# Reordering the first batch's bank reads and moving loads between DMA queues, in a spectral filter and gated feed-forward kernel

## The chip, the cores and the metric

The kernel runs on one core of a Trainium2 chip. A core has a matrix engine (TensorE, PE in the profile), VectorE (DVE), ScalarE (ACT), GpSimd (POOL) and SyncE (SP), and 16 DMA engines that SP, ScalarE and GpSimd feed through queues of their own (SP's and ScalarE's are q1 and q10 in the profile, GpSimd's q0). The metric is the device time of one execution in microseconds (us); the time of a kernel is the median of its runs.

## The reference

`x` has 8 batches of 3008 rows of 256 values. Each column is filtered in the frequency domain, and the result goes, row by row, through a gated feed-forward block with 1536 hidden columns:

```python
X = np.fft.rfft(x, axis=1)
y = np.fft.irfft(X * (filt_r + 1j * filt_i)[None], n=3008, axis=1)
t = y.reshape(8 * 3008, 256)
out = (np.maximum(t @ w_gate, 0) * (t @ w_val)) @ w_out
```

## The kernel before, in words

The sequence of 3008 is factored as 94 x 32, and the transform becomes matrix products in three stages.

**Stage A** is a transform of length 94, an fp32 product with the table `WA`. For batch 0 it is `first_a`, whose result VectorE transposes into `AT`. For batch 1 it is `items_a`: 16 items, four to each of four parts c. Each item is one product into a bank `psA` and one copy into `asb`; after four items a part is stored to the DRAM buffer `Abuf`. Batch 1's `Abuf` is then read back by `load_at`, in four parts, as the tile `at`. Batches from 2 on do stage A in another way (`load_chunk`, `fold_chunk`, `tiled_a`), which the change leaves alone.

**Stage B** works in six steps i. `fwd` makes two banks `psX` (e = 0 and 1). `product` multiplies each bank with the real and with the imaginary filter table (`Ftr` for k = 0, giving `tt`; `Fti` for k = 1, giving `uu`), four products to a step. `inv` turns `tt` and `uu` of a step into two banks `psD`, and copies them into `dsb`, which goes in a few stores to the DRAM buffer `Dbuf`. For seven of the 24 products of batch 0, listed in `POOL_U`, ScalarE first copies the bank into an fp32 tile `xs` and GpSimd multiplies that copy; VectorE does the rest from the bank. Within step i the order written out is `fwd(i)`, `inv(i-2)`, the products, and then what `amid(i)` puts in: some of the items A of batch 1, taken one by one from the generator `early`.

**Stage C** (`item_c`) reads `Dbuf` back in four slabs z (`load_d`, tile `dC`), multiplies with `M1`, and gives `yT`, a block of 512 rows of the filtered sequence, transposed.

**The feed-forward loop** takes 47 blocks of 512 rows. For each block there are 12 steps `gv` with the products `psV` and `psG` (L485), a copy of `psV` by ScalarE (L488) and a product by VectorE (L490). `o_part` multiplies the block before with `WoT` (L504). From here on, the work of the other stages is hung at given steps of the loop by `at_step`.

Each engine takes its instructions in the order in which the program writes them. Loads into the weights `WvT`, `WgT` and `WoT` go by GpSimd's queue (`load_vg`, by columns, and `load_o`). `hold_gpsimd` is a tiny copy on GpSimd that reads some tile; what stands behind it on GpSimd is held until that tile is written. Half of each filter table's rows are a copy of the other half (`place_filter`, made with an engine's copy or with a DMA).

Before the feed-forward loop starts the program writes, in order: the first B with its items A, `load_d` of slabs 0 and 1, a hold of GpSimd until slab 0 is there, the second half of `WvT` and `WgT`, the items A that are left with `item_c` of block 0 among them, a hold until `yT` is there, `WoT`. `load_at` of batch 1 is at steps 0 to 3 of the loop, slabs 2 and 3 at steps 9 and 14, all on SP's queue.

Of the kernel before, what the change touches and what calls it, by code (L numbers as in the profile page):

```python
# [35 lines left out]
def _ap(t, offset_elems, ap_list):  # L36
    return dataclasses.replace(
        t, offset=t.offset + offset_elems, ap=[list(p) for p in ap_list]
    )
# [81 lines left out]
def kernel(  # L121
# [10 lines left out]
    nc = tc.nc  # L132
    B, S_, D = x.shape
    DFF = moe_w_gate.shape[1]
# [4 lines left out]
    NZ = 4  # L139
# [95 lines left out]
    def place_filter(fi, a, half, copy):  # L235

        dst = FILT[fi][1]
        gs = slice(H * half, H * half + H)
        r = a * 64
        copy(dst[r + 32:r + 64, gs, :], dst[r:r + 32, gs, :])  # L240

    def place_nyq():
        for (src, dst), n in zip(FILT, nyq):
            nc.vector.tensor_copy(dst[96:97, NG - 1, :], n)

    def load_vg(c0, c1):
        for (w_hbm, w_sb) in ((moe_w_val, WvT), (moe_w_gate, WgT)):
            nc.gpsimd.dma_start(w_sb[:, :, c0:c1],
                                _ap(w_hbm, c0, [[DFF, 128], [128 * DFF, 2], [1, c1 - c0]]))

    def load_o():
        for c in range(2):
            nh = NFT // 2
            nc.gpsimd.dma_start(WoT[:, c * nh:(c + 1) * nh],
                                _ap(moe_w_out, c * nh * 128 * D, [[D, 128], [128 * D, nh], [1, D]]))

    def hold_gpsimd(tile_):

        scr = sb.tile([128, 8], FP32, tag="scr", bufs=2)
        nc.gpsimd.tensor_copy(scr[:tile_.shape[0]], tile_)  # L260
# [101 lines left out]
    POOL_U = ((0, 1), (1, 0), (1, 1), (2, 0), (2, 1), (3, 1), (4, 0))  # L362
    ats = {}

    def load_at(b, c):
        if c == 0:
            ats[b] = sb.tile([128, NG, D], BF16, tag="at", bufs=1, name="at")
        nc.sync.dma_start(ats[b][c:c + 125:4],
                          _ap(Abuf[b], c * NROW * NC2 * D, [[D, 32], [4 * NC2 * D, NG], [1, D]]))

    psXs, tus, dsbs = {}, {}, {}
# [15 lines left out]
    def product(b, i, e, k, pool=False):  # L387

        psX = psXs[b, i, e]
        pool_, bufs = (fs, 4) if b else (pro, 6)  # L390
        p = pool_.tile([128, 2, D], BF16, tag=("tt", "uu")[k], bufs=bufs, name=("tt", "uu")[k])
        filt = (Ftr, Fti)[k][:, 4 * i + e:4 * i + 4:2, :]
        if pool:
            xs = pro.tile([128, 2, D], FP32, tag="xs", bufs=3)
            nc.scalar.copy(xs, psX)
            nc.gpsimd.tensor_tensor(p, xs, filt, op=ALU.mult)
        else:
            nc.vector.tensor_tensor(p, psX, filt, op=ALU.mult)  # L398
        tus[b, i, e, k] = p

    def inv(b, i, tags=None, cuts=CUTS):

        if i in cuts:
            dsbs[b] = i, sb.tile([128, 2, 4, D], BF16, tag="dsb", bufs=3, name="dsb")
        i0, dsb = dsbs[b]
        psD = [ps.tile([128, 2, D], FP32, tag=tags[a] if tags else fft_tag(), name="psD")
               for a in range(2)]
        for m in range(2):
            for k in range(2):
                for a in range(2):  # L410
                    for e in range(2):
                        nc.tensor.matmul(psD[a][64 * e:64 * e + 64, m],  # L412
                                         (I2t, I2u)[k][64 * a:64 * a + 64, 4 * i + 2 * m + e, :],
                                         tus[b, i, e, k][64 * a:64 * a + 64, m],
                                         start=(k == 0), stop=(k == 1),
                                         tile_position=(64 * a, 64 * e))
        o = 2 * (i - i0)
        for a in range(2):
            nc.scalar.copy(dsb[:, a, o:o + 2, :], psD[a])  # L419
        if i + 1 in cuts:  # L420
            nc.sync.dma_start(_ap(Dbuf[b], 2 * i0 * D, [[NG * D, 128], [NG // 2 * D, 2], [1, (o + 2) * D]]),
                              dsb[:, :, :o + 2, :])

    def first_b(amid):

        cuts = (0, 2, 4, 5, 6)
        for i in range(6):
            fwd(0, i)
            if i > 1:
                inv(0, i - 2, cuts=cuts)  # L430
            for e in range(2):
                product(0, i, e, 0)
                product(0, i, e, 1, pool=(i, e) in POOL_U)
            amid(i)
        inv(0, 4, cuts=cuts)
        amid(6)
        inv(0, 5, cuts=cuts)

    dCs = {}

    def load_d(b, z0=0, z1=NZ):
        for z in range(z0, z1):
            dC = sb.tile([NROW, 8, D], BF16, tag="dC", bufs=6)
            for e in range(2):
                nc.sync.dma_start(dC[48 * e:48 * e + 48],
                                  _ap(Dbuf[b], (64 * e + 16 * z) * NG * D,
                                      [[D, 48], [48 * D, 8], [1, D]]))
            dCs[b, z] = dC
# [13 lines left out]
    def item_c(k, h):  # L462

        if h == 0:
            yTs[k] = sb.tile([128, 2, W], BF16, tag="yT", bufs=3, name="yT")
        tag = fft_tag() if k == 0 else ("psv", "psg")[h]
        psY = ps.tile([128, W], FP32, tag=tag, name="psY")
        for (o, b, n2, n1, w) in runs(k * W, W):
            nc.tensor.matmul(psY[:, o:o + w],  # L469
                             dCs[b, n2 // 8][:, n2 % 8, h * 128:(h + 1) * 128], M1[:, n1:n1 + w],  # L470
                             start=True, stop=True)
        dst = yTs[k][:, h]
        if h == 0:
            nc.scalar.copy(dst, psY)  # L474
        else:
            nc.vector.tensor_copy(dst, psY)  # L476
# [57 lines left out]
    def warm(n, cols=512):  # L534

        psJ = ps.tile([128, 512], FP32, tag=fft_tag(True), name="psJ")
        for i in range(n):
            nc.tensor.matmul(psJ[:, :cols], junk[:, 0:128], junk[:, :cols], start=True, stop=True)
# [36 lines left out]
        turn_a(h)  # L575
    for i in range(12):
        warm(2)
    place_filter(1, 1, 0, nc.scalar.copy)
    place_filter(1, 0, 0, nc.vector.tensor_copy)
    for half in range(2):  # L580
        for a in range(2):
            place_filter(0, a, half, nc.sync.dma_start)
# [8 lines left out]
    def amid(i):  # L591
        if i == 3:
            place_nyq()
        for _ in range((1, 1, 1, 2, 1, 2, 1)[i]):
            next(early)()

    hold_gpsimd(AT[0:32, NG - 1, D - 8:])
# [1 line left out]
    turn["tags"], turn["side"] = ("fft", "psv", "psg"), "pso"  # L599
    first_b(amid)  # L600
    turn["tags"], turn["side"] = ("fft", "psv", "psg", "pso"), None
    load_d(0, 0, 2)
    hold_gpsimd(dCs[0, 0][:, 7, D - 8:])
    for c in range(2, 4):
        load_vg(c * DFF // 4, (c + 1) * DFF // 4)
    for i, f in enumerate(early):
        f()
        if i == 5:
            for h in range(2):
                item_c(0, h)  # L610
    hold_gpsimd(yTs[0][:, 0, 0:8])
    load_o()
    prologue.close()
    fs = ctx.enter_context(tc.tile_pool(name="fs", bufs=2))
    XP = []
# [9 lines left out]
    def at_step(s, f):  # L625
        side.setdefault(s, []).append(f)

    for s, z in ((9, 2), (14, 3)):
        at_step(s, lambda z=z: load_d(0, z, z + 1))
    C_AT = (8, 10)  # L630
    at_step(2, clear_chunks)
    for b in range(1, B):
        end = (b * S // W - 1) * NFT + C_AT[0] - 5
        if b == 1:
            for c in range(4):
                at_step(c, lambda c=c: load_at(1, c))
        else:
            for j, e in enumerate((-74, -69, -62, -55) if b == 2 else (-74, -69, -64, -57)):
                l = (22, 29, 34, 43)[j] if b == 2 else end - 115 + NFT * j

                def next_x(b=b, j=j, l=l):
                    hold_gpsimd(prods[-1][:, 0:8])
                    load_chunk(b, j)
                    if j:
                        fold_chunk(b, j - 1)
                    if j == 3:
                        fold_chunk(b, j)
                at_step(l, next_x)
                at_step(end + e, lambda b=b, j=j: tiled_a(b, j))
            at_step(end + e + 4, lambda b=b: load_at_tiled(b))  # L650
        for i in range(7):
            l = -35 + 5 * i if b == 1 else -40 + 6 * i
            if i < 6:
                at_step(end + l, lambda b=b, i=i: fwd(b, i))
                for h in range(4):
                    at_step(end + l + h, lambda b=b, i=i, h=h: product(b, i, h // 2, h % 2))
            if i > 0:
                at_step(end + l, lambda b=b, i=i: inv(b, i - 1, ("psv", "psg")))
        at_step(end - 2, lambda b=b: load_d(b))
# [42 lines left out]
```

## Time and profile before

| | |
|---|---|
| median of 3 runs | 891.98 us (891.27 to 892.26) |
| the profiled execution's own time | 891.01 us |
| its span | 889.2 us |
| TensorE busy | 866.7 us, 97% |
| VectorE, ScalarE, GpSimd busy | 572.9, 500.0 and 365.3 us |
| mean granted clock of TensorE | 0.997 |

The profile is of one execution. Its span runs from the first to the last instruction, and the execution's own time has 1.8 us around it. Busy shares are averages over the whole span. What a change in one stage is worth is read from that stage, so most readings here are of the stretch from 20 to 80 us, in which the first B ends and the feed-forward loop begins.

### The profile page before, as it was taken

How to read it: one execution, taken by the hardware profiler on the slowest of the kernel's cores; microseconds unless marked ns; L12 is line 12 of the kernel's file. 1: busy time of each engine (PE TensorE's matmuls, PEld its weight loads, DVE VectorE, ACT ScalarE, POOL GpSimd, SP SyncE). 2: the span in 40 equal slices, each digit the busy share in tenths (PEclk: the TensorE clock that was granted, in tenths of full speed). 3: DMA queues.
4: the chain of work that ended last, by engine and by line, in shares of the span. 5: the costliest groups of instructions: out<-in, count | busy, mean ns of one | idle time of the engine just before them, and what ended most of it. 6: DMA issues, size and time to landing. Idle time of an engine off the chain costs nothing.

```text
span 889.2 us, 18975 instructions
## 1 busy us (share of the span) xinstructions
PE 866.7 (97%) x7065; PEld 506.8 (57%) x7186; DVE 572.9 (64%) x871; ACT 500.0 (56%) x889; POOL 365.3 (41%) x361
## 2 busy tenths in 40 slices
PE   8889999999999999999999999999999999999997
PEld 3335555556556665566655665556555556566665
DVE  4837766577666776667765676657776577655553
ACT  4655555555655566556565556555655555555553
POOL 4450697138651577316771176802867000000001
PEclk9999999999999999999999999999999999999999
DMA  9994556534556337453376334763446512321111
GB/s 242 289 234 83 158 138 154 128 104 118 130 139 134 105 101 157 125 124 96 106 184 133 84 104 110 176 138 82 118 134 149 122 31 80 89 67 36 37 31 53
DMA packets 110769, 107.26 MB, mean 121 GB/s; under 512 B 20167, under 2 KB 95463, under 8 KB 110038
## 3 DMA queue, kind: packets, MB, share of 16 engines
q1 hardware_dynamic: 86998, 78.20, 34.5%
q0 software_dynamic: 22960, 26.40, 12.1%
q10 hardware_dynamic: 720, 1.45, 0.5%
q8 instruction: 56, 0.92, 0.4%
q14 instruction: 35, 0.29, 0.1%
HBM read 60.42 MB, written 48.23 MB: 122 GB/s over the span
## 4 chain that ended last, share of the span: by engine, by line
PE 86%; DVE 4%; ACT 4%; DMA 3%; issue 2%; POOL 0%; SPq 0%; DVEq 0%; POOLq 0%; ACTq 0%
PE psG L485 27%; PE psO L504 25%; PE psV L485 25%; DVE prod L490 3%; PE psF L341 3%; ACT vsb L488 3%; PE psD L412 2%; PE psX L382 2%; PE psY L469 2%; DMA Ftr<-Ftr 1%; DMA Ftr<-in_filt_r_dram 1%; PE psA L294 1%; DMA dC<-Dbuf 1%; DMA XF<-in_x_dram 1%; ACT dsb L419 0%
## 5 line engine op out<-in xcount | busy, mean ns | idle before, releaser
L490 DVE SCALAR_TENSOR_TENSOR prod<-psG,vsb 128x512 bf16<-128x512 f32 x564 | 389.3, 690 | 263.4 <-ACT vsb L488 254.5
L488 ACT CAST vsb<-psV 128x512 bf16<-128x512 f32 x564 | 332.3, 589 | 262.9 <-PE psV L485 176.5
L485 PE MATMUL psG<-yT,WgT 128*128 128x512 bf16 x1107 | 331.0, 379 | 6.9 <-DVE prod L490 0.8
L504 PE MATMUL psO<-WoT,prod 128*128 128x256 bf16 x2256 | 336.4, 273 | 1.1
L485 PE MATMUL psV<-yT,WvT 128*128 128x512 bf16 x1030 | 315.8, 380 | 0.5 <-ACT asb L348 0.5
L504 PEld LDWEIGHTS <-prod 128*128 128x128 bf16 x2256 | 220.6, 98 | 143.5
L485 PEld LDWEIGHTS <-WgT 128*128 128x128 bf16 x1128 | 110.1, 98 | 136.5 <-issue 3.6
L485 PEld LDWEIGHTS <-WvT 128*128 128x128 bf16 x1128 | 98.8, 98 | 42.3 <-issue 31.1
L260 POOL CAST scr<-prod 128x8 f32<-128x8 bf16 x24 | 4.6, 191 | 256.4 <-DVE prod L490 256.4
L527 POOL DMA_DIRECT2D out_dram<-osb x5 | 2.6, 538 | 195.9 <-ACT osb L517 195.9
L517 ACT COPY osb<-psO 128x512 f32<-128x512 f32 x92 | 54.0, 586 | 27.9 <-PE psO L504 26.5
L398 DVE TENSOR_TENSOR tt<-psX,Ftr 128x512 bf16<-128x512 f32 x96 | 65.1, 682 | 0.9 <-PE psX L382 0.9
L327 POOL TENSOR_TENSOR fold<-XP 128x1024 f32<-128x1024 f32 x24 | 56.5, 2356 | 19.7 <-PE psF L341 19.5
L398 DVE TENSOR_TENSOR uu<-psX,Fti 128x512 bf16<-128x512 f32 x89 | 60.6, 681 | 0.0
L419 ACT CAST dsb<-psD 128x512 bf16<-128x512 f32 x96 | 51.6, 589 | 13.1 <-PE psD L412 13.1
L314 POOL DMA_DIRECT2D XP<-in_x_dram x96 | 56.9, 598 | 3.0 <-PE psY L469 1.5
L328 POOL TENSOR_TENSOR XP<-XP 128x1024 f32<-128x1024 f32 x24 | 56.4, 2350 | 1.9
L348 ACT CAST asb<-psF 128x512 bf16<-128x512 f32 x48 | 25.8, 589 | 30.5 <-PE psF L341 30.5
L348 DVE CAST asb<-psF 128x512 bf16<-128x512 f32 x48 | 30.9, 686 | 18.6 <-PE psF L341 18.6
L474 ACT CAST yT<-psY 128x512 bf16<-128x512 f32 x47 | 27.6, 586 | 26.4 <-PE psY L469 26.2
L469 PE MATMUL psY<-M,dC 96*128 96x94 bf16 (+18 forms) x604 | 37.5, 198 | 4.1 <-DMA dC<-Dbuf 4.0
L476 DVE CAST yT<-psY 128x512 bf16<-128x512 f32 x47 | 32.0, 681 | 11.6 <-PE psY L469 11.6
(76 smaller groups left out, 492.4 us busy)
## 6 DMA issues: line engine op xcount, KB each, us to landing
dC<-Dbuf SPq DMA_DIRECT2D x64, 192.0 KB
XP<-in_x_dram POOLq DMA_DIRECT2D x48, 256.0 KB, 6.0
Dbuf<-dsb SPq DMA_DIRECT2D x23, 512.0 KB
at<-Abuf SPq DMA_DIRECT2D x28, 384.0 KB
XP<-in_x_dram POOLq DMA_DIRECT2D x96, 96.0 KB, 2.7
Abuf<-asb SPq DMA_DIRECT2D x96, 96.0 KB
out_dram<-osb SPq DMA_DIRECT2D x69, 94.0 KB
XF<-in_x_dram SPq DMA_DIRECT2D x15, 256.0 KB
```

Source lines behind the costliest of these rows:

```text
L314: nc.gpsimd.dma_start(xp[r:r + 24, 0:4:2, :], _ap(x, (b * N1 * N2 + o) * D, [[N2 * D, 24], [47 * N2 * D, 2], [1, 512]]))
L327: tt(t, xp[:, 0:2], xp[:, 2:4], op=ALU.add)
L328: tt(xp[:, 2:4], xp[:, 0:2], xp[:, 2:4], op=ALU.subtract)
L348: copy(asf[:, :, q, :], banks[q])
L398: nc.vector.tensor_tensor(p, psX, filt, op=ALU.mult)
L419: nc.scalar.copy(dsb[:, a, o:o + 2, :], psD[a])
L469: nc.tensor.matmul(psY[:, o:o + w], dCs[b, n2 // 8][:, n2 % 8, h * 128:(h + 1) * 128], M1[:, n1:n1 + w], start=True, stop=True)
L485: nc.tensor.matmul(pt[:, :W], w[:, h, ft * 128:(ft + 1) * 128], yt[:, h, :], start=(h == 0), stop=(h == 1))
L488: nc.scalar.copy(vsb, psV[:, :W])
L490: nc.vector.scalar_tensor_tensor(prod, in0=psG[:, :W], scalar=0.0, in1=vsb, op0=ALU.max, op1=ALU.mult)
L504: nc.tensor.matmul(psO[:, t % 2], prods[ft][:, t * 128:(t + 1) * 128], WoT[:, ft, :], start=(ft == 0), stop=(ft == NFT - 1))
L517: copy(osb[:, t0 % 2:t % 2 + 1], psO[:, t0 % 2:t % 2 + 1])
```

## The change

Six edits go together.

1. One of the four copies that fill the lower half of `Fti` for the first half of the columns (`place_filter(1, 0, 0)`) is made by a DMA on ScalarE's queue; VectorE made it.
2. In a step of the first B, the order of the four products depends on which of them GpSimd makes. Where it makes one of a bank, ScalarE's copy `xs` of that bank is written first and VectorE's product from the bank after it, where the two share a bank.
3. In the last step of the first B, the copy of `psD` for a = 0 is made by VectorE; ScalarE made both.
4. `amid(6)` no longer takes an item A. One more is left for after the first B, and `item_c` of block 0 comes after seven of these where it came after six.
5. The third quarter of `WvT` and `WgT` and the first part of `at` are loaded by GpSimd's queue at the end of step 5 of the first B.
6. After the first B only slab 0 goes by SP's queue. Slab 1, the last quarter of `WvT` and `WgT`, the second part of `at`, `WoT`, the third and fourth parts of `at`, and slabs 2 and 3 go by GpSimd's queue in this order, with a hold ahead of slab 1 (until slab 0 is there) and one ahead of `WoT` (until `yT` is there).

```diff
     def load_at(b, c):
...
-        nc.sync.dma_start(ats[b][c:c + 125:4],
+        nc.gpsimd.dma_start(ats[b][c:c + 125:4],
...
         for a in range(2):
-            nc.scalar.copy(dsb[:, a, o:o + 2, :], psD[a])
+            copy = nc.vector.tensor_copy if (b, i, a) == (0, 5, 0) else nc.scalar.copy
+            copy(dsb[:, a, o:o + 2, :], psD[a])
...
-            for e in range(2):
-                product(0, i, e, 0)
-                product(0, i, e, 1, pool=(i, e) in POOL_U)
+            on_pool = [(i, e) in POOL_U for e in range(2)]
+            seq = {(0, 0): ((0, 0), (0, 1), (1, 0), (1, 1)), (0, 1): ((1, 1), (0, 0), (0, 1), (1, 0)),
+                   (1, 0): ((0, 1), (1, 0), (1, 1), (0, 0)), (1, 1): ((0, 0), (1, 1), (0, 1), (1, 0))}
+            for e, k in seq[tuple(map(int, on_pool))]:
+                product(0, i, e, k, pool=k == 1 and on_pool[e])
...
-    def load_d(b, z0=0, z1=NZ):
+    def load_d(b, z0=0, z1=NZ, eng=nc.sync):
...
-                nc.sync.dma_start(dC[48 * e:48 * e + 48],
+                eng.dma_start(dC[48 * e:48 * e + 48],
...
+    place_filter(1, 0, 0, nc.scalar.dma_start)
     place_filter(1, 1, 0, nc.scalar.copy)
-    place_filter(1, 0, 0, nc.vector.tensor_copy)
...
-        for _ in range((1, 1, 1, 2, 1, 2, 1)[i]):
+        if i == 5:
+            load_vg(DFF // 2, 3 * DFF // 4)
+            load_at(1, 0)
+        for _ in range((1, 1, 1, 2, 1, 2, 0)[i]):
...
-    load_d(0, 0, 2)
+    load_d(0, 0, 1)
     hold_gpsimd(dCs[0, 0][:, 7, D - 8:])
-    for c in range(2, 4):
-        load_vg(c * DFF // 4, (c + 1) * DFF // 4)
+    load_d(0, 1, 2, nc.gpsimd)
+    load_vg(3 * DFF // 4, DFF)
     for i, f in enumerate(early):
         f()
-        if i == 5:
+        if i == 6:
             for h in range(2):
                 item_c(0, h)
+    load_at(1, 1)
     hold_gpsimd(yTs[0][:, 0, 0:8])
     load_o()
+    for c in range(2, 4):
+        load_at(1, c)
+    load_d(0, 2, 4, nc.gpsimd)
...
-    for s, z in ((9, 2), (14, 3)):
-        at_step(s, lambda z=z: load_d(0, z, z + 1))
...
-        if b == 1:
-            for c in range(4):
-                at_step(c, lambda c=c: load_at(1, c))
-        else:
+        if b > 1:
```

## The prediction, made before the result was known

> **What bounds the kernel now.** The page comes first: TensorE is busy nearly everywhere.
>
> ```profile
> PE 866.7 (97%) x7065; PEld 506.8 (57%) x7186; DVE 572.9 (64%) x871; ACT 500.0 (56%) x889; POOL 365.3 (41%) x361
> PE   8889999999999999999999999999999999999997
> ```
>
> The feed-forward loop starts with L485 at 57 us; after that TensorE's waits are small (waits by engine: 1.2 us in 56 to 130, 0.8 us later). All the changed code runs before or just after that start. So the end moves by as much as the first psV moves, plus whatever new wait appears in the first dozen steps. The chain of waits around that start:
>
> ```profile
> 43.83 1.05 ACT dsb L419 x2
> 44.88 0.55 ACT asb L297
> ...
> 45.45 1.07 ACT dsb L419 x2
> ...
> 46.54 2.43 DMA Dbuf<-dsb
> ...
> 49.06 0.33 SPq L445
> ...
> 49.44 5.09 DMA dC<-Dbuf
> ...
> 54.66 0.62 PE psY L469 x12
> 55.28 1.78 PE psA L294 x2
> 57.06 0.85 PE psV L485 x2
> ```
>
> The order is: last copy of the first B (to 46.52), store of D, load of D's first slab (to 54.53), psY, one item A, psV. TensorE runs out of items A at 50.7 and idles 3.97 us. The table of windows (sum, then PE, PEld, DVE, ACT and POOL busy, granted clock, DMA share, GB/s) shows the after-effect:
>
> ```profile
> 51.80:55.20 3.40, 0.54 (x13) 0.57 (x14) 0.00 (x0) 0.11 (x1) 0.28 (x2) 1.00 1.21 231
> 55.20:58.60 3.40, 3.18 (x9) 1.03 (x8) 0.69 (x1) 1.30 (x3) 3.40 (x6) 0.50 1.20 280
> 58.60:62.00 3.40, 3.40 (x17) 1.50 (x16) 2.29 (x4) 2.16 (x5) 3.40 (x4) 1.00 1.28 237
> ```
>
> The clock column is to be seen: one stretch of 3.4 us at 0.50. In it the item took 1.78 us instead of 0.9 and the first psV 0.85 instead of 0.43; with 0.22 of issue the price is about 1.5 us.
>
> Inside the first B the timeline shows who reads a bank first:
>
> ```profile
> 30.63 3.07 DVE L398 TENSOR_TENSOR tt<-psX,Ftr 128x512 bf16<-128x512 f32 x5
> 31.35 0.59 ACT L395 COPY xs<-psX 128x512 f32<-128x512 f32 x1 [3.71 <-DVE tt L398]
> 33.22 0.30 PE L412 MATMUL psD<-uu,I2u 64*64 64x256 bf16 x3 [0.94 <-POOL uu L396]
> ```
>
> ScalarE's xs waited 3.71 us for VectorE's tt on the same bank, GpSimd started late, and TensorE waited 0.94 us for its uu. A second such wait, 0.66 us for xs, comes at 35.87.
>
> **What the Trainium skill says.** "PSUM — Partial Sum Buffer", section "PSUM bank collisions raise a hardware error": two engines must not access one bank and quadrant together, reads included. The trace agrees (xs at 31.35, tt's end at 31.31). So in the new order VectorE waits for ScalarE where ScalarE waited before. "DMA: Bandwidth & Descriptors", section "Issuing engines are not separate DMA queues": all queues share 16 engines and interleave. Partly agreed: in 54 to 58.5 us SP's queue took 120.5% and none of GpSimd's packets, although GpSimd issued at 55.11; a GpSimd load starts late beside a full SP queue. "TensorE: Matmul & The Clock Gate", part 1: an idle window of about 3.4 us halves the clock, and the window is free-running. The trace agrees: 0.50 for 3.4 us.
>
> **The change part by part.** Spacings from the timeline: VectorE 0.60 us, ScalarE 0.48 in a run, GpSimd's product 1.16, an item A 1.03 and each further one 0.86, the 16 matmuls of inv 0.56.
>
> *Filter copy to ScalarE's queue.* VectorE's copy (28.45, 0.95 us) goes; the first tt comes at 28.92, when psX is there, instead of 29.43. ScalarE issues one DMA, about 0.55 us like SP's Ftr<-Ftr, after its last AS copy (23.53), before the Fti data that its next copy waits for (24.89): nothing is late behind it. Landing is not shown for this queue at this load. High bound: Ftr<-Ftr, 6.27 us, 29.8; low: 3.2 us, 26.7; I take 27.5. The first uu would run at 29.5; by the next step VectorE has 1.6 us to spare, so even the high end costs nothing. A GpSimd product needs it at 30.8 only.
>
> *Order of bank reads.* GpSimd is held by its two weight issues until 30.84, so uu(0,1) starts there instead of at 32.02: ready at 32.0 instead of 33.2. inv 0 ends at 32.6, its two dsb copies run 32.66 to 33.73, and only then does ScalarE reach xs(2,1): 33.62 to 34.21. VectorE's tt(2,1), at 33.0 before, now waits for that and ends at 34.93; this eats the 0.5 us from above. inv 1 gets past its banks at 34.97 (35.87 before): 0.9 us ahead. Next xs(3,1) ends at 37.09, tt(3,1) at 37.81, inv 2 at 38.4, 0.7 us ahead. Then dsb of inv 2 (38.4 to 39.5), xs(4,0) to 39.97, and last tt(4,0) to 40.69; inv 3 needs that bank, and before it had waited for xs(4,0) to 40.76. The lead is gone: **items 6 and 7 start at 41.28 as against 41.26**. If VectorE need not wait, 0.7 us would stay; if ScalarE's queue is fuller than I count, up to 0.5 us is lost.
>
> *One item fewer, one copy to VectorE.* Item 8 no longer stands between inv 4 and inv 5 (43.71 to 44.73): inv 5 runs 43.75 to 44.35, right when the last uu is ready (43.69). Its copies: VectorE 44.39 to 45.07, ScalarE after inv 4's copies, 44.79 to 45.38 (its asb of item 8 is out of the way). Last store issued at **45.4 instead of 46.54: 1.1 us ahead**. Item 8 is not saved; it now fills the wait for D, so items end at 50.5 instead of 50.7.
>
> *Loads moved to GpSimd.* After its last product (41.2) GpSimd issues two weight loads (0.74 and 0.71) and at(1,0), which waits for the Abuf store issued at 38.5 on SP; that queue drains at about 42 to 43.5, so at(1,0) is issued at about 44. Nothing compute-like stands behind it until the hold on D's slab. Their data runs beside the last D stores, which had the engines alone: SP's packets took 78.7% of 43.5 to 49. The weights (2 x 192 KB, by the rate of 36 to 40 us, 0.68 MB at 94.6% of 4 us) cost 2.2 us of all engines; at(1,0), 384 KB at 1.19 MB in 4.5 us, 1.4 us. Up to 1 us fits into the quiet 42 to 43.5. From both sides: if all of it fits into gaps, the last store lands 1.1 us ahead (47.9); if all stands ahead of it, 1.1 ahead, 3.6 behind, about 0.3 lost overlap: 51.5. I take 49.8, 0.8 us later than 48.97.
>
> *D's slab alone.* In 49 to 51 us ScalarE's Abuf store held the engines (74.1%, no packet of SP's); it still is issued at 48.7 and drains at 51.8 to 52. Then 384 KB of dC, at 0.73 MB in 3.5 us, take 1.9 us; no second slab and no at follow in that queue. Before, data of those came in before the slab's landing (0.73 MB by 54.5, where the slab is 0.39). Landing: **53.7 instead of 54.53**, bounds 53.0 and 55.6. The Abuf store is why the exact landing of D's store matters little.
>
> *After the start.* SP loses ten loads and keeps only outputs there: nothing gained, since at and the late slabs had no waiter. GpSimd's order is now slab 1, weights' last quarter, at(1,1), WoT, at(1,2), at(1,3), slabs 2 and 3, then 7.1 us of memset ending near 72; the next thing behind it is the hold at step 22, at 86 us: free. Due times with psV at 56.2: slab 1 at step 8, 63; last quarter at step 9, 64; WoT at step 12, 69; at(1) at step 16, 75; slab 2 at step 20, 80. By 0.17 to 0.25 MB/us slab 1 lands at 60, the quarter at 62 to 63, WoT at 66 to 69.5: covered, thinly. If that cover goes, each late microsecond is a TensorE wait.
>
> **Sum.** psY at 53.85 instead of 54.66: 0.8 us ahead; the idle stretch is 3.35 us instead of 3.97, so I leave the cold stretch in. The profiled execution took 891.01 us (span 889.2), 0.97 under the median 891.98. Profiled: 891.01 - 0.8 = 890.2; **median 891.2**. A measurement of this kernel can tell about 0.2%, 1.8 us, from no change.
>
> **Rivals.**
> *The clock stays up.* The idle stretch falls to about 3.4 us, the length of the gate's window, so a window holding mostly idle is less sure. For it: before, the window still had 0.54 us of work. Against: 3.35 us is no safe distance. Worth 0.8 + 1.5 = 2.3 us: 889.7.
>
> *GpSimd's single queue is late* (slower side). At the slow rate seen for its loads in 60 to 68 us (1.35 MB in 8 us at 118.8%), slab 1, quarter, at(1,1) and WoT are 1.92 MB: 11.4 us from a first packet at 58 (issued 54.3, and the GpSimd loads issued at 55.11 began 3.6 us later) is 69.4, with ScalarE's last Abuf store (1.1 us) 70.5, against WoT's due time 69. It decides from the point where the WoT halves land after 69 and 70.3. Place: the first psO, or psV of step 9. Price: 1 to 3 us of wait, and with the D store at its late bound (0.3 lost instead of 0.8 won) 1.5 to 3.5 over: median 894.0.
>
> *The slab doesn't move.* ScalarE's Abuf store and rest of at(1,0) hold it to 54.5: 892.0.
>
> **Numbers.** Likeliest case 0.34, clock up 0.31, single queue late 0.22, no move 0.13. Range 888.9 to 894.2. Faster by over 0.2%: 0.32 (clock up, and a little of the likeliest); within: 0.45; slower: 0.23.
>
> **What would show it.** Right: first tt at 28.9; VectorE waiting over 1 us for xs around 33 to 34; last Dbuf store issued at 45 to 45.7, its landing over 3 us later; dC waited for until 53 to 54.5. Wrong: no wait of VectorE on xs and the store issued before 44.9; the store landing before 48.5 (GpSimd's loads cost nothing); TensorE waiting for WvT, WgT or WoT after 60; a clock of 1.00 throughout 50 to 60.

## The result, and the profile after

| | before | after |
|---|---|---|
| median | 891.66 us (891.27 to 893.39, 6 runs) | 896.49 us (894.93 to 901.06, 6 runs) |
| profiled execution, its span | 891.01, 889.2 us | 896.73, 894.9 us |

After over before is 1.0056, with a 95% interval of 1.0032 to 1.0079: **slower**, by some 5 us, and outside the range that was given. Neither the likeliest case (0.8 us faster), nor the one with the clock up, nor the one in which the slab doesn't move came about. The slower rival had the sign, but its place was the weights after the start, and there TensorE waits for none of them.

TensorE's own waits in the trace of the kernel after, from 20 to 130 us (us in total, times, the longest):

```profile
PE psY L472 <- DMA dC<-Dbuf: 5.3, 1, 5.3
PE psA L294 <- DMA XF<-in_x_dram: 2.6, 1, 2.6
PE psD L412 <- DVE tt L398: 0.9, 1, 0.9
```

In before the wait for D's slab (dC) was 3.97 us, and a wait for x (XF) was not among them. No line names WvT, WgT or WoT, so the weights are not where the time went. The first item A in before:

```profile
29.04 1.07 PE L294 MATMUL psA<-XF,WA 128*96 128x512 f32 x2 [0.16 <-PE psX L382]
```

The chain of waits of after has both places (start, us, what):

```profile
23.37 7.51 DMA XF<-in_x_dram
30.88 0.25 issue
31.12 1.07 PE psA L294 x2
...
46.23 0.59 ACT dsb L420
46.82 0.22 SPq L422
47.15 6.64 DMA Dbuf<-dsb
53.80 0.33 SPq L448
54.18 3.28 DMA dC<-Dbuf
57.59 1.01 PE psY L472 x12
58.60 1.83 PE psA L294 x2
60.44 0.85 PE psV L488 x2
```

The chain now runs back through an x load: the first item A starts at 31.12 instead of 29.04. The last store of D is issued at 47.15 (before 46.54) and takes 6.64 us to land (before 2.43). The slab alone takes 3.28 us (before 5.09). psY starts 2.93 us later, psV 3.38 later. By the series of psO instructions the loss is 4.2 us at the first (74.39 against 70.17) and 4.6 at the last (888.89 against 884.31): the loop has given nothing back and lost little.

The last 1.1 us of the difference in span lie behind the last psO: 4.9 us of before, 6.0 of after. There GpSimd's closing wait (DRAIN, the longest of three) is 2 us longer, first in before, then in after:

```profile
L697 POOLq DRAIN  x3: 103/193/4607, 882.9 to 888.8; - x3
L702 POOLq DRAIN  x3: 46/103/6618, 887.5 to 894.6; - x3
```

That is no chance of one execution. In the nine traces of kernels that load at of batch 1 and slabs 2 and 3 by GpSimd's queue (after, e1, e2, e3, e5, e6, e8, e9 and e13 below) the stretch is 5.9 to 6.0 us and the wait 6.5 to 6.6; in the five that don't (before, e4, e10, e11, e12) they are 4.7 to 4.9 and 4.6. So that part of edit 6 brings some 1.1 us at the very end. Why the closing wait grows is not shown.

The table of windows, with the columns as before, shows the clock around the idle stretch:

```profile
53.70:57.10 3.40, 0.00 (x0) 0.00 (x0) 0.00 (x0) 0.00 (x0) 0.00 (x0) 1.00 0.41 124
57.10:60.50 3.40, 2.90 (x15) 1.55 (x16) 0.69 (x1) 0.61 (x2) 2.52 (x5) 0.50 0.26 75
60.50:63.90 3.40, 3.18 (x8) 1.21 (x8) 0.69 (x1) 1.73 (x3) 3.40 (x6) 0.50 0.90 131
```

A gap of 5.27 us left two windows at 0.50 where 3.97 us left one. The second window goes with the step from 2.93 us at psY to 4.2 at the first psO. The length of the gap doesn't fix the number: in the kernels below 5.19 us (e1) left one and 3.30 us (e5) two.

### The profile page after: what moved, and what is told of

Same layout as the page of the kernel before. It is cut to its first block, busy times and chain, and to the rows that moved or that the text cites. A ratio compares the mean times of both kernels' runs of the same rounds, so it can differ in the third digit from the quotient of the medians.

```text
span 894.9 us, 18982 instructions
## 1 busy us (share of the span) xinstructions
PE 867.8 (97%) x7065; PEld 507.6 (57%) x7186; DVE 573.3 (64%) x871; ACT 499.5 (56%) x888; POOL 370.6 (41%) x371
## 4 chain that ended last, share of the span: by engine, by line
PE 86%; DVE 5%; ACT 4%; DMA 3%; issue 1%; POOL 0%; SPq 0%; DVEq 0%
PE psG L488 26%; PE psO L507 25%; PE psV L488 24%; DVE prod L493 4%; ACT vsb L491 3%; PE psF L341 3%; PE psD L412 2%; PE psX L382 2%; PE psY L472 2%; DMA XF<-in_x_dram 1%; PE psA L276 1%; DMA Dbuf<-dsb 1%; PE psA L294 1%; DMA out_dram<-osb 0%; DMA dC<-Dbuf 0%
## 5 line engine op out<-in xcount | busy, mean ns | idle before, releaser
L477 ACT CAST yT<-psY 128x512 bf16<-128x512 f32 x47 | 27.5, 586 | 28.1 <-PE psY L472 27.9
L472 PEld LDWEIGHTS <-dC 96*128 96x128 bf16 x604 | 34.8, 98 | 10.1 <-DMA dC<-Dbuf 6.1
```

The costliest lines, as they stand in the source:

```text
L472: nc.tensor.matmul(psY[:, o:o + w], dCs[b, n2 // 8][:, n2 % 8, h * 128:(h + 1) * 128], M1[:, n1:n1 + w], start=True, stop=True)
```

## The experiments

Each time is set against runs of the kernel before on the same chip, and the ratio is given with its 95% interval. A whole profile of one execution starts some tenths earlier or later by chance (the first psX of these traces lies between 28.1 and 29.2), so places are counted from the first psX. "Store" is the issue of D's last store, "flight" is its time to landing, "slab" the slab's load, from the issue of its second half to the landing. Waits are those of TensorE for weights.

| kernel | ratio | store | flight | slab | psY | waits for weights |
|---|---|---|---|---|---|---|
| before | 1 | 18.07 | 2.43 | 5.09 | 26.19 | 0 |
| after | 1.0056 (1.0032 to 1.0079) | 19.07 | 6.64 | 3.28 | 29.51 | 0 |
| e4, edit 1 only | 1.0028 (1.0018 to 1.0038) | 21.87 | 2.4 | 5.43 | 30.23 | 0 |
| e10, two filter DMAs | 1.0029 (1.0018 to 1.0039) | 21.66 | 2.4 | 5.19 | 29.84 | 0 |
| e1, after without edit 1 | 1.0023 (1.0012 to 1.0034) | 17.21 | 6.48 | 3.30 | 27.58 | 0 |
| e5, also at(1,0) held | 0.9999 (0.9991 to 1.0007) | 17.21 | 4.60 | 3.29 | 25.69 | 0 |
| e3, after without 1 and 5 | 1.0005 (0.9996 to 1.0014) | 17.21 | 3.60 | 4.22 | 25.62 | 1.9 |
| e9, quarter ahead of slab 1 | 1.0006 (0.9998 to 1.0014) | 17.20 | 3.6 | 4.22 | 25.6 | 4.5 |
| e6, without 1, 2 and 5 | 1.0005 (0.9997 to 1.0014) | 17.56 | 3.3 | 5.00 | 26.46 | 1.8 |
| e2, after without 5 | 1.0049 (1.0035 to 1.0063) | 19.92 | 3.6 | 4.41 | 28.45 | 2.5 |
| e8, edit 6 only | 1.0014 (1.0001 to 1.0027) | 18.17 | 2.42 | 4.61 | 25.79 | 0.3 |
| e11, edits 3 and 4 only | 0.9994 (0.9982 to 1.0006) | 17.05 | 3.32 | 5.55 | 26.52 | 0 |
| e12, and an Abuf store moved | 1.0001 (0.9990 to 1.0013) | 17.06 | 3.54 | 3.44 | 24.64 | 2.7 |
| e13, and at and slabs behind WoT | 0.9979 (0.9970 to 0.9988) | 17.06 | 3.54 | 3.52 | 24.72 | 0 |

**Edit 1: the filter copy as a DMA.** e1 is after with VectorE making the copy again; e4 is before with the DMA alone.

```diff
# e1, against after
-    place_filter(1, 0, 0, nc.scalar.dma_start)
     place_filter(1, 1, 0, nc.scalar.copy)
+    place_filter(1, 0, 0, nc.vector.tensor_copy)
# e4, against before: the same lines the other way round
```

> The changed kernel with edit 1 alone taken back: VectorE makes the filter copy again. Theory (two separate costs: the filter DMA on ScalarE's queue delays the loads of x, and the early GpSimd loads delay D's last store): the first item A starts at 29 us instead of 31.1, the last Dbuf store is issued at about 46 instead of 47.15, still takes about 6 us to land, and the time is 1 to 1.5 us under the changed kernel's: about 895. Rival 1 (the early GpSimd loads are the whole loss, the late items A are made up for anyway): as the changed kernel, 896.5. Rival 2 (the new order of bank reads is what makes the store late): the store is still issued at about 47, 896.5.

> The kernel before with edit 1 alone: the filter copy is a DMA on ScalarE's queue. Theory: the first item A starts at about 31 instead of 29.0, the last store is issued 1 to 2 us later than the 46.54 of before, the time is 1 to 2 us over the kernel before: about 893.3. Rival 1: the late item is made up for within the first B, 891.7 as before. Rival 4 (the x loads were late for another reason, such as GpSimd's or SP's own loads): first item at 29.

Taken back, the edit gives 0.33% (1.0056 to 1.0023, about 2.9 us); alone it costs 0.28% (2.5 us), both more than was expected. By the intervals the first is known to some 0.26%, the second to 0.10%. VectorE is not the reason. In after the DMA is issued at 22.60 and lands at 29.92, VectorE's first uu waits 0.83 us for it, and the chain of waits doesn't pass there. What it holds up is on another queue: the third x load, which the first item A reads, lands at 30.88 instead of 28.95. The windows of before, and then of after, while both are in flight (last columns: clock, DMA share, GB/s):

```profile
26.00:27.00 1.00, 1.00 (x6) 0.47 (x5) 1.00 (x1) 1.00 (x1) 0.00 (x0) 1.00 0.96 309
27.00:28.00 1.00, 1.00 (x6) 0.29 (x3) 1.00 (x1) 0.63 (x1) 0.00 (x0) 1.00 1.05 434
```

```profile
26.00:27.00 1.00, 1.00 (x6) 0.47 (x5) 1.00 (x1) 1.00 (x1) 0.00 (x0) 1.00 0.98 197
27.00:28.00 1.00, 0.65 (x4) 0.10 (x1) 1.00 (x1) 0.63 (x1) 0.00 (x0) 1.00 0.91 213
```

The engines are about as busy as before and carry little more than half as much (a mean of 205 GB/s against 372; in e4 the two windows have 248 and 266). From 25 to 29 us SP's queue moved 0.69 MB where in before it moved 1.36, while the copy's 0.20 MB on ScalarE's queue took 31% and then 14% of the engines' time. What SP's queue moves in a given window isn't the same in both: the fast windows of the x loads (434 and 406 GB/s from 27 to 29 in before) come later in after (320 and 418 from 29 to 31). How much each single packet is slowed is not shown. The waits of e4 and then of e1:

```profile
PE psA L294 <- DMA XF<-in_x_dram: 2.7, 1, 2.7
```

```profile
PE psA L294 <- DMA XF<-in_x_dram: 0.7, 1, 0.7
```

The wait comes with the DMA and shrinks without it. It isn't zero without it: the ten traces that have no such DMA show 0 to 1.4 us, the four that have one 1.9 to 3.6. x arrives only just in time. In e4 the gap also put TensorE's clock down for two windows (30.80 to 37.63), and its store comes later for it; in after's own trace the clock stayed up there.

e10 makes ScalarE's copy a DMA too, as a double dose on the kernel before.

```diff
+    place_filter(1, 0, 0, nc.scalar.dma_start)
-    place_filter(1, 1, 0, nc.scalar.copy)
-    place_filter(1, 0, 0, nc.vector.tensor_copy)
+    place_filter(1, 1, 0, nc.scalar.dma_start)
```

> The kernel before with two of the filter copies as DMAs on ScalarE's queue (VectorE's and ScalarE's copy), where the fourth run of the call before had one. Theory (a copy within SBUF of 192 KB on a second queue holds up the loads of x by about 2 us each): the first item A starts at 33 to 34 us instead of 31.7 with one and 29.0 with none; time 1.5 to 3 us over that with one, about 897.5. Rival (the x loads are late for another reason, and the DMA only coincides): first item still at about 31.5, 895.

The first item A starts at 32.88, which is 4.05 us behind the first psX, where e4 has 3.12 (31.73). So the place gives way further, by 0.9 us and not by 1.3 to 2.3; but the time is that of e4 (1.0029 against 1.0028). In its trace one window of the first B is cold where e4 has two, and so the store comes no later. That is a reading of one execution each; the price by dose is not shown.

**Edit 5: GpSimd's early loads.** e3 is e1 with edit 5 taken back as well (weight quarter and at(1,0) come after the hold, behind slab 1). e5 keeps the quarter early and holds only at(1,0).

```diff
# e3, against e1                      (e5: only the two load_at lines)
-        if i == 5:
-            load_vg(DFF // 2, 3 * DFF // 4)
-            load_at(1, 0)
...
     load_d(0, 1, 2, nc.gpsimd)
+    load_vg(DFF // 2, 3 * DFF // 4)
     load_vg(3 * DFF // 4, DFF)
...
+    load_at(1, 0)
     load_at(1, 1)
```

> The changed kernel with edits 1 and 5 both taken back. Theory: the two costs add; store issued at 45.5 to 46, landed by 48.5, slab 0 at 52 to 53, about 1.5 us under the second run of this call and 0.5 to 2 us under the kernel before: about 890.5. Rival 2 (bank order costs too): store issued at 46.5 or later, the time at or above the kernel before, 892.

> The changed kernel with edit 1 taken back and, of edit 5, only the first part of at (it goes behind the hold; the third quarter of the weights stays early). Theory (each early GpSimd load takes engine time from D's last stores): with half of the early bytes the last store takes 4.5 to 5.5 us to land, between the 6.5 seen with both and the 3.6 seen with none; the weights are there in time, so TensorE waits for no weight after 58 us; time about 893.5, between 893 and 894.6. Rival (the at load is harmless, the weights do it all): landing still 6 us or more.

The chains of e1, of e5 and of e3:

```profile
45.98 6.48 DMA Dbuf<-dsb
...
52.92 3.30 DMA dC<-Dbuf
```

```profile
46.04 4.60 DMA Dbuf<-dsb
...
51.09 3.29 DMA dC<-Dbuf
```

```profile
46.21 3.60 DMA Dbuf<-dsb
...
50.27 4.22 DMA dC<-Dbuf
```

Issued at the same place, the store takes 3.60 us with neither load ahead of it, 4.60 with the quarter (384 KB in two loads), 6.48 with at(1,0) (384 KB) as well. From e3 to e5 the landing slips by 0.8 us, but the slab is there at 54.49 and 54.38: something else holds it. From e5 to e1 the landing slips by 1.8 us, and the slab comes at 56.22. The times agree: at(1,0) early costs 0.24% (0.9999 to 1.0023, about 2.1 us), the quarter early costs nothing in sum, since without it TensorE waits 1.9 us for weights. e3, which was expected 0.5 to 2 us under before, is no faster than before.

So after's 0.56% comes off in two steps: 0.33% with the filter DMA and 0.24% with at(1,0). What is left, e5, is the kernel before within 0.1%. It still has the longer end (6.0 us), so what is left of the change must give about 1 us back elsewhere, an estimate from these two figures; the traces, one execution each, don't tell where.

e2 undoes edit 5 in after and leaves the filter DMA.

> The changed kernel with edit 5 alone taken back: the third quarter of the weights and the first part of at are issued by GpSimd only after the hold on slab 0, behind slab 1. Theory: the last store is still issued at about 47.1, but lands some 2.5 us later instead of 6.6; slab 0 is there at 53 to 54, TensorE is cold for one window and not two; the time is 4 to 5 us under the changed kernel's: about 892. Rival 1: the same gain or more. Rival 3 (the store is slow because it is issued close behind two other stores of SP's queue, not because of GpSimd): the store still takes over 5 us, about 896.

The 4 to 5 us that were expected of it did not come. At 1.0049 it can't be told from after: with the x loads late, the flight falls to 3.6 us, but the waits for weights (2.5 us) come in its place, and its trace has a cold window in the first B.

**What holding the loads costs.** e3's waits:

```profile
PE psG L488 <- DMA WgT<-in_moe_w_gate_dram: 1.2, 1, 1.2
PE psV L488 <- DMA WvT<-in_moe_w_val_dram: 0.7, 1, 0.7
```

This is the rival "GpSimd's single queue is late", in a kernel whose first psV comes at 56.01. In after it comes at 60.23, and the same queue is in time. e9 puts the third quarter ahead of slab 1 in e3's order:

```diff
+    load_vg(DFF // 2, 3 * DFF // 4)
     load_d(0, 1, 2, nc.gpsimd)
     load_vg(3 * DFF // 4, DFF)
```

> The changed kernel with edits 1 and 5 taken back, and behind the hold on slab 0 the third quarter of the weights goes ahead of slab 1. Theory (without the early load TensorE waited 0.75 us for WvT and 1.21 us for WgT, because slab 1 stood ahead of them on GpSimd's queue): these two waits go or fall under 0.7 us together, slab 1 still comes before step 8, and the time falls by 1 to 2 us from 893.4 to about 891.9, 0.5 to 1.5 us under the kernel before. Rival (the weights are late because GpSimd's loads as such are slow): the waits stay above 1.3 us, 893.4.

```profile
PE psO L507 <- DMA WoT<-in_moe_w_out_dram: 2.1, 2, 1.7
PE psV L488 <- DMA WvT<-in_moe_w_val_dram: 2.0, 1, 2.0
PE psG L488 <- DMA WgT<-in_moe_w_gate_dram: 0.4, 1, 0.4
```

The wait did not go, it moved down the queue to WoT. (The profiled execution was 3 us over the median of its runs: read the places, not the sizes.) Another order within the queue doesn't remove the wait. That the limit is what the queue has to carry by 70 us is the likely reading, not tested by itself.

**Edit 2: the order of bank reads.** e6 is e3 with the old order.

```diff
-            for e, k in seq[tuple(map(int, on_pool))]:
-                product(0, i, e, k, pool=k == 1 and on_pool[e])
+            for e in range(2):
+                product(0, i, e, 0)
+                product(0, i, e, 1, pool=(i, e) in POOL_U)
```

> The changed kernel with edits 1 and 5 taken back, and edit 2 too (the old order of bank reads). Theory (edit 2 swaps one wait for another, so it is worth nothing): TensorE's waits in the first B for VectorE's tt (0.9 us) go, waits of 0.9 us for uu and 0.7 us for xs come back; the last store is issued within 0.4 us of 46.2; time as with the new order, 893.4 +- 0.7. Rival (the new order costs): 1 us or more faster. Rival (the new order gains): last store issued at 47 or later, 894.4 or more.

Both have 1.0005. (The two orders were compared only with edits 1 and 5 taken back.) Timeline of after, VectorE and then TensorE:

```profile
35.98 0.69 DVE L398 TENSOR_TENSOR tt<-psX,Ftr 128x512 bf16<-128x512 f32 x1 [1.34 <-ACT xs L395]
```

```profile
36.72 0.30 PE L412 MATMUL psD<-tt,I2t 64*64 64x256 bf16 x2 [0.90 <-DVE tt L398]
```

In the new order VectorE stands 1.34 us behind ScalarE's xs, and TensorE waits for VectorE's tt (0.9, and 0.3 for uu) where in e6 it waits for xs and GpSimd's uu (0.7 and 0.5). The edit exchanges waits and brings nothing that can be measured.

**Edits 3 and 4, and who holds the slab.** e11 is before with these two alone; no load is moved. e12 adds one line: the third Abuf store goes from ScalarE's queue to SP's, where it is issued behind D's slabs.

```diff
# e11, against before
-            nc.scalar.copy(dsb[:, a, o:o + 2, :], psD[a])
+            copy = nc.vector.tensor_copy if (b, i, a) == (0, 5, 0) else nc.scalar.copy
+            copy(dsb[:, a, o:o + 2, :], psD[a])
...
-        for _ in range((1, 1, 1, 2, 1, 2, 1)[i]):
+        for _ in range((1, 1, 1, 2, 1, 2, 0)[i]):
...
-        if i == 5:
+        if i == 6:
# e12, against e11
-                eng = nc.scalar if c > 1 else nc.sync
+                eng = nc.scalar if c > 2 else nc.sync
```

> The kernel before, with only the two edits inside the first B that bring D's last store forward: one item A fewer between inv 4 and inv 5, and the last copy of inv 5 split between VectorE and ScalarE. No load is moved. Theory (the prediction's step, with GpSimd's early loads away): last store issued at 45.3 to 45.6, landed 2.4 to 3.6 us later, at 47.9 to 49; the slab's load is then held by ScalarE's Abuf store, which is issued near 48.7 as before, so psY comes only 0.3 to 0.8 us ahead: 0.3 to 1.2 us under before, and 1.5 more if the clock stays up. Rival (the item's place gives back what it takes, or the landing takes 3.6 us): psY within 0.3 us of before, time within 0.5 us of before. Rival (nothing holds the slab): psY 1.1 us ahead or more, idle gap about 3 us, no cold stretch, 2 to 3 us under before.

> The same two edits as the run of edits 3 and 4, and in addition the third Abuf store goes from ScalarE's queue to SP's, where it stands behind D's slab loads. Theory (that store, in flight from 48.7 to 52, takes the engines from the slab's load): the slab lands 1 to 1.5 us earlier than with the two edits alone, psY at 52.3 to 53, idle gap under 3.2 us, TensorE's clock 1.00 throughout 50 to 60, 1.5 to 3 us under before. Rival (the slab's load is limited by its own descriptors or by the second slab beside it, not by that store): psY as with the two edits alone, the same time as that run within 0.4 us.

The chains of e11 and of e12:

```profile
46.05 3.32 DMA Dbuf<-dsb
...
49.83 5.55 DMA dC<-Dbuf
...
55.52 1.01 PE psY L470 x12
```

```profile
46.01 3.54 DMA Dbuf<-dsb
...
50.01 3.44 DMA dC<-Dbuf
...
53.59 0.62 PE psY L470 x12
```

The gain expected of e11 did not come. Its store is issued 1.02 us ahead (17.05 against 18.07), and nothing of it reaches psY: 0.9 us goes in the flight (this store, now 0.6 us behind the one before it and not 1.6, takes 3.32 us where that of before took 2.43), and the rest in the slab's load. (Its profiled execution was the slowest of its 13, by a wait of 2.4 us that ends at 183 us, so only the start is read.) With the Abuf store out of the way, the same slab, with slab 1 beside it as before, takes 2.1 us less. **ScalarE's Abuf store holds the slab**: moving that one transfer brings the slab's load to 3.44 us without touching a load. after, e1 and e5 come to the same (3.28 to 3.30 us) in another way: their slab is issued so late that this store is nearly through. In before it lands 3.0 us behind the slab's issue, in e3 2.7, in these three 0.7 to 1.3. In all nine traces where it lands 2.7 us or more behind, the slab takes 4.2 to 5.6 us.

But e12 is no faster, where 1.5 to 3 us were expected. Its timeline on TensorE, 19 us later:

```profile
73.00 0.58 PE L505 MATMUL psO<-WoT,prod 128*128 128x256 bf16 x2 [2.58 <-DMA WoT<-in_moe_w_out_dram]
73.38 1.06 PE L486 MATMUL psV<-yT,WvT 128*128 128x512 bf16 x2
```

The 1.9 us won at psY are lost at WoT. Its second half lands at 72.96 where in before it lands at 69.26. From issue to landing the halves of WoT take, in e12 and then in before:

```profile
DMA to landing us min/median/max: 11.7/13.4/15.1
DMA to landing us min/median/max: 8.7/9.5/10.4
```

What SP's queue has beside it is at and the slabs 2 and 3, the last of them issued by 65.9 us in e12 and by 69.1 in before, so more of them is ahead of WoT's end; e13 tests this. The gap puts the clock down (the next instructions take twice their time).

**Edit 6 alone**, e8: before, with slab 0 on SP's queue and all else on GpSimd's behind it.

```diff
-    load_d(0, 0, 2)
+    load_d(0, 0, 1)
     hold_gpsimd(dCs[0, 0][:, 7, D - 8:])
-    for c in range(2, 4):
-        load_vg(c * DFF // 4, (c + 1) * DFF // 4)
+    load_d(0, 1, 2, nc.gpsimd)
+    load_vg(DFF // 2, 3 * DFF // 4)
+    load_vg(3 * DFF // 4, DFF)
...
+    load_at(1, 0)
+    load_at(1, 1)
     hold_gpsimd(yTs[0][:, 0, 0:8])
     load_o()
+    for c in range(2, 4):
+        load_at(1, c)
+    load_d(0, 2, 4, nc.gpsimd)
```

> The kernel before, with the late half of the change alone: D's first slab alone on SP's queue, everything else on GpSimd's behind it in order of need (slab 1, weight quarters 3 and 4, at(1,0), then WoT, the rest of at, slabs 2 and 3). The filter copy, the order of banks, the items and the first B are those of before. Theory (the slab's load is shortened, but GpSimd's single queue is late): last store issued at 46.4 to 46.6 and landed at 49 as before, the slab's load about 3.3 us where it was 5.1, so psY 1 to 1.8 us ahead (53 to 53.7), and then 1.5 to 3 us of waits of TensorE for WgT, WvT or WoT between 58 and 75, since two quarters stand behind slab 1: time 0 to 1.5 us over before. Rival (the slab was held by ScalarE's Abuf store and not by what stands beside it): psY at 54.5 as before and the same waits for weights: 1.5 to 3 us over before. Rival (GpSimd's queue keeps up): no waits of TensorE over 0.5 us there, 1 to 3 us under before.

The slab's load falls only to 4.61 us (the Abuf store is still there), psY comes 0.4 us ahead, and the waits for weights are 0.3 us, not 1.5 to 3. The time, 0.14% over before (about 1.2 us), is within what was expected, the waits were not. In its trace the first psO is 0.5 us late, the last 1.6 and the end 2.7: 1.1 us lie behind the last psO, the longer end that comes with at and the slabs on GpSimd's queue. The 1.1 us within the loop have no one wait to name; that part stays open.

**A version faster than both**, e13: e12 with at(1) and the slabs 2 and 3, the part of edit 6 that e12 lacked, on GpSimd's queue behind WoT. Slab 1 stays on SP, and the weights stay first on GpSimd.

```diff
     load_o()
+    for c in range(4):
+        load_at(1, c)
+    load_d(0, 2, 4, nc.gpsimd)
...
-    for s, z in ((9, 2), (14, 3)):
-        at_step(s, lambda z=z: load_d(0, z, z + 1))
...
-        if b == 1:
-            for c in range(4):
-                at_step(c, lambda c=c: load_at(1, c))
-        else:
+        if b > 1:
```

> The run with the third Abuf store on SP's queue, and in addition all of at(1) and D's slabs 2 and 3 go from SP's queue to GpSimd's, behind WoT; slab 1 stays on SP, the weights' last two quarters stay first on GpSimd. Theory (in the run before this one the 1.9 us won at the first psV were given back where WoT's second half landed at 72.96 instead of 69.26, held up by at and the slabs that SP issued beside it, and the wait of 2.58 us put TensorE's clock down): with those behind WoT, the weights' last quarter lands by 61.5 and WoT by 66 to 69, TensorE waits less than 0.5 us for any load between 55 and 75, no cold stretch before 800, first psO near 68.7, last psO 1.5 to 2 us ahead of before, time 1.5 to 2.5 us under before. Rival (the gain is given back at the next load: at(1) for the items at step 16, due near 73.5, or a slab at step 20): a wait of TensorE on tt, AT or dC of 1 to 3 us between 73 and 82, time within 1 us of before. Rival (GpSimd's own issuing, 16 more issues of 0.7 us, makes its memset and the holds after it late): time over before, with waits of TensorE near 86 to 95.

Its ratio is 0.9979 (0.9970 to 0.9988): 891.24 us median of 21 runs, beside 893.06 for before on that chip, as expected. It has the longer end as well (5.9 us behind the last psO). From 20 us to the end, TensorE waits for a DMA three times:

```profile
PE psY L470 <- DMA dC<-Dbuf: 2.5, 1, 2.5
PE psA L294 <- DMA XF<-in_x_dram: 0.8, 1, 0.8
```

```profile
PE psX L382 <- DMA at<-Abuf: 0.4, 1, 0.4
```

WoT lands at 68.62, 10.5 us from its issue, and nobody waits for it, nor for at(1) or the late slabs. The 0.4 us are at 178 us, at the same place of batch 2 where e11's execution waited 2.4. One cold window is still there (54.26, after a gap of 2.49 us); in e12 a gap of 2.41 us left none.

## Why the prediction was wrong, step by step

None of the signs that the prediction named for being wrong came: they watched the bank reads, the store's landing, the weights and the clock. Two of its signs for being right failed: the store was issued at 47.15 (not by 45.7), and dC was waited for until 57.5 (not 54.5). The loss came from a transfer that it had called free and from a sum that it had discounted.

**Filter copy to ScalarE's queue: the first step that failed.** The landing (27.5 taken, 26.7 to 29.8) was 29.92, at the high end; VectorE waited 0.83 us for it, which the chain of waits doesn't show as a cost. "Even the high end costs nothing" was wrong, since only the readers of the copied data were asked about. The DMA takes part in the same 16 engines as the x loads, and the first item A had no slack for those: counted from the first psX it starts at 3.04 us in after and 3.12 in e4 where before has 0.57, some 2.5 us, and the time loses 2.5 to 2.9. The Trainium skill's page "DMA: Bandwidth & Descriptors", section "Issuing engines are not separate DMA queues", which the prediction used for the loads at 54 us, bears on this one too; the trace agrees with its x loads 1.9 us late on another queue.

**Order of bank reads: right, as far as it was tested.** A wait of VectorE on xs of over 1 us and no gain: 1.34 us, and e6 equals e3 within 0.1%.

**One item fewer, one copy to VectorE: right in size, wrong in place.** 1.1 us ahead was worked out, e11 has 1.02. In after the store was issued at 47.15 and not at 45.4, because the items had started late.

**Loads moved to GpSimd: the second step that failed, a term mis-sized.** The flight of the last store was taken as 4.4 us (45.4 to 49.8). With both loads it is 6.48 (e1) and 6.64 (after). What failed is the discount, that about half of what the early loads cost fits into gaps. The prediction's own terms for the worst case (2.43 in before, 3.6 for the loads, 0.3 of lost overlap) give a flight of 6.3 us, which is close; from 48.97, with the store 1.1 ahead, they lead to 51.8 and not to the 51.5 that it wrote. Among the terms, the "lost overlap" was put at 0.3 us and is 0.9 to 1.2 (2.43 against 3.3 to 3.6 in every kernel with edits 3 and 4 and no early load), at(1,0) was put at 1.4 us and adds 1.9, and the quarter, put at 2.2, adds 1.0: the errors nearly cancel.

**D's slab alone: right as far as the Abuf store reaches.** That its store makes the exact landing matter little holds from 49.81 to 50.64 (e3, e5), and fails once the landing is past it: at 52.46 in e1 and 53.79 in after. From the store's landing to the slab's the step used 3.9 us (49.8 to 53.7); after has 3.67 (53.79 to 57.46).

**After the start: right for after, thin as it said, and without a term for the end.** No wait for weights where everything is 3 us late; 1.8 to 4.5 us of them in e3, e6 and e9, which start in time with these loads held, but only 0.3 in e8. That GpSimd's extra issues are free was wrong at the very end, where they go with 1.1 us.

**The clock.** One cold stretch was left in for 3.35 us; two came with 5.27. The Trainium skill's page "TensorE: Matmul & The Clock Gate", part 1, has the window as free-running. The traces agree, since the length of a gap alone doesn't decide: gaps of 2.41 and 3.24 us (e12, e3) left no cold window, 2.49, 3.97 and 5.19 us (e13, before, e1) left one, 3.30 and 5.27 us (e5, after) two. By that account it was luck, in each single execution, how a gap fell into the windows.

## What to carry to other kernels

A DMA in place of an engine's copy isn't free because its readers have slack: list what else is in flight in its window, and ask which of those has a reader that waits. For a transfer that must land soon, look for the one transfer of another queue that shares its time, and not only at its neighbours in its own queue: here one store moved by one line gave 2.1 us at the slab, and edit 6 alone 0.5. And a start brought forward is kept only when the next transfer down the line, here WoT, is brought forward with it; here that took putting what is needed later behind it in the same queue. Last, look at the end of the kernel too when issues move to another engine: nothing in the stretch that was changed showed the 1.1 us there.

## What was not expected of the hardware

With a copy of 192 KB from SBUF to SBUF in flight beside x loads of 256 KB, the engines carried 197 and 213 GB/s in two windows where they had carried 309 and 434 at a like busy share, and the third x load landed 1.9 us later. One load of 384 KB issued ahead of a store of 256 KB added 1.9 us to its landing, although the two were on different queues. In e12 a WoT load that lands in 10.4 us in before and 10.5 in e13 took 15.15 us; the at and slab loads of SP's queue, which e13 moves behind it, are what it had beside it. And GpSimd's closing wait was 4.6 us in five kernels and 6.5 to 6.6 in the nine with ten or eight more loads on its queue, a difference with no overlap.
